# Second token chunk transposed by DMA instead of TensorE, first loads in another order, and two additions placed between scaling pieces

## Chip, core and metric

One NeuronCore of a Trainium2 chip runs the whole kernel. The metric is the device time of one execution in microseconds (us), lower is better. Engines are named as in the profile: PE is TensorE (matmuls), PEld its weight loads, DVE is VectorE, ACT is ScalarE, POOL is GpSimd; SP is SyncE, which here only issues DMAs. A name with a q (SPq, DVEq) is the engine's sequencer. L12 is line 12 of the kernel before.

## What is computed

2048 tokens of width 1024, bfloat16. A gate mixes two branches: a dilated local attention (8 keys per query, distance 2) and a gated feed-forward of width 3584.

```python
x = A_x                                                   # [1, 2048, 1024]
g = sigmoid((x * gate_w).sum(-1, keepdims=True))
q, k, v = split(x @ wqkv)                                 # 32 heads of 32
a = softmax_over_8_keys(q, k) @ v  ->  heads joined  @ wo
b = (gelu(x @ w_gate) * (x @ w_up)) @ w_down
out = g * a + (1 - g) * b
```

## The kernel before, in words

**Layout.** All matmuls contract over partitions, so x is needed transposed: features on the partitions, tokens along the row. The 2048 tokens are four chunks of 512, c = 0 to 3. A transposed chunk has eight slices (kt = 0 to 7) of 128 features by 512 tokens. Chunks 0 and 1 form `xf[0]` (tiles `c1`, `c2`), chunks 2 and 3 form `xf[1]`. Chunks 0 and 1 are loaded as they stand (`load_xn`, L141) and transposed on PE, 32 transposes of 128 x 128 each, with eight copies out of PSUM shared by DVE (L219) and ACT (L217) (`pe_transpose_chunk`, L208). Chunks 2 and 3 are transposed by DMA: 16 transposing DMAs of 512 tokens x 128 features from SP (L340).

**Units.** After a plain start (`plain_pair`, L240: the first 256 gate and up columns for chunks 0 and 1 by ordinary matmuls), projections run as "units" (class `Unit`, L360) with seven block products instead of eight (a Strassen-Winograd scheme). A unit has five PE steps. `p1` and `p5` are 4 matmuls each, `p26` is 8, `p73` is 8, `p4` is 4. PE's order is p1 of unit b, p73 of unit b-1, p5 and p26 of unit b, p4 of unit b-1. Between p73 and p4 of the same unit DVE reads the two PSUM banks with L403, and p4 adds into one of those banks, so p4 has to wait for L403. The units need sums and differences of the x blocks (`x_forms`, L196, line L199: T1 = R12 - R11, T2 = R22 - T1, T4 = R21 - T2, where R11 and R21 are slices 0-3 and 4-7 of the pair's first chunk, R12 and R22 those of its second) and of the weights (`sums_pair`, L318; `sums_qk`, L456, line L463). DVE makes the forms of `xf[1]` early, between the unit work of `xf[0]` (`late_forms`, L780).

**Order of the work.** Every engine runs its instructions in program order, written out by hand at the start and then by a planner: background DVE tasks with priorities and due units are cut into the units by credits (`run_bg`, L442). Loads are issued by SP, in order; stores by POOL. SP's order at the start: chunk 0, first weight pair in two column halves (`load_pair(raw0, 0, True)`, L172), chunk 1, second weight pair (L174), four q/k weight blocks of 1 MB (L336), 16 DMA transposes (L340), and then loads of `w_down` pieces (L860).

**End.** The second half of the down projection (`down(1)`, L1066) runs two-level block products (`level2`, L1037). For this half DVE makes all forms: `scale_task` (L918) multiplies a block of A by (1 - g) in three pieces of four slices, `comb_task` (L927) adds or subtracts blocks, `forms_L` and `forms_R` (L1004, L1012) make the inner sums. `join` (L1031) adds an inner product that is kept in SBUF to two PSUM banks, for i = 0 and i = 1; both wait for a product of PE. `pieces`, `take(g, k)` and `run` draw the next steps of such a chain: `rest` at L1093 holds the three scaling pieces of A21 and then the five pieces of AD = A11 - A21.

## Time and profile before

| | |
|---|---|
| median of 3 runs | 720.85 us (720.46 to 720.87) |
| profiled execution: its time, its span | 720.8 us, 719.0 us |
| PE busy | 707.4 us (98% of the span) |
| DVE busy | 673.0 us (94%) |
| ACT, POOL busy | 328.5 us, 134.1 us |
| moved by DMA | 162 MB, 225 GB/s mean |

A profile page gives the busy time of each engine, its load over the span in 40 slices, and groups of instructions by line: how many, mean length, and how long the engine stood idle before them and for whom. The timeline lists instructions in order of start, neighbours of a kind merged (x8); a number in brackets is idle time before, with the engine that ended it. A DMA line of SPq is the issue alone, the data land later. The two numbers at the head of a timeline row are start and length in us.

### The profile page before, as it was taken

What the parts mean: (1) busy time and instruction counts of PE and PEld (TensorE: products, weight loads), DVE (VectorE), ACT (ScalarE), POOL (GpSimd) and SP (SyncE); (2) the same over time, 40 slices, a digit from 0 to 9 for tenths busy, and PEclk for the clock granted to TensorE, in tenths of its full rate; (3) what the DMA queues carried; (4) which work ended last, traced back from release to release, by engine and by line L of the source; (5) the groups of instructions that cost most, each with busy time, mean ns of one, the idle gap of its engine ahead of it and who ended that gap; (6) DMA issues with size and microseconds to landing.
All of it is one profiled execution on the core that took longest, in us unless ns stands there. A gap on an engine that the chain in (4) does not pass through costs nothing. (4 is left out here: it accounts for less than half of the span.)

```text
span 719.0 us, 10748 instructions
## 1 busy us (share of the span) xinstructions
PE 707.4 (98%) x4051; PEld 408.3 (57%) x4107; DVE 673.0 (94%) x721; ACT 328.5 (46%) x600; POOL 134.1 (19%) x233
## 2 busy tenths in 40 slices
PE   8999999999999999999999999999999999999997
PEld 4466656655544444444444444444447886758886
DVE  2789989999999999999999999999999999899997
ACT  4554546444456665555555555555322321231421
POOL 1323544133210332121200000000210002110011
PEclk9999999999999999999999999999999999999999
DMA  9976743278264758574935746371891799995941
GB/s 276 283 176 227 229 142 133 98 248 303 100 206 128 234 190 254 171 227 142 294 111 155 279 134 210 120 285 59 314 421 60 301 405 399 422 427 217 379 196 60
DMA packets 91748, 162.04 MB, mean 225 GB/s; under 512 B 19264, under 2 KB 68320, under 8 KB 87344
## 3 DMA queue, kind: packets, MB, share of 16 engines
q1 hardware_dynamic: 74992, 105.46, 43.0%
q0 software_dynamic: 15984, 48.29, 19.3%
q10 hardware_dynamic: 720, 7.60, 2.7%
q8 instruction: 32, 0.52, 0.3%
q14 instruction: 20, 0.16, 0.1%
HBM read 112.17 MB, written 54.14 MB: 231 GB/s over the span
## 5 line engine op out<-in xcount | busy, mean ns | idle before, releaser
L366 PE MATMUL banks<-arena 128*128 128x512 bf16 x2136 | 472.1, 379 | 4.2 <-DVE arena L403 0.7
L366 PEld LDWEIGHTS <-arena 128*128 128x128 bf16 x2184 | 240.4, 111 | 235.3 <-issue 7.0
L1046 PE MATMUL banks<-arena 128*128 128x256 bf16 x1260 | 138.7, 273 | 0.6 <-DVE arena L1012 0.6
L1046 PEld LDWEIGHTS <-arena 128*128 128x128 bf16 x1260 | 123.1, 98 | 16.4 <-issue 1.1
L403 DVE TENSOR_TENSOR arena<-banks,arena 128x1024 bf16<-128x1024 f32 x78 | 95.2, 1221 | 11.0 <-PE banks L366 5.4
L389 ACT COPY arena<-banks 128x512 f32<-128x512 f32 x78 | 45.7, 586 | 130.8 <-PE banks L366 130.8
L374 ACT CAST arena<-banks 128x512 bf16<-128x512 f32 x102 | 59.6, 584 | 42.4 <-PE banks L366 42.4
L745 DVE TENSOR_TENSOR arena<-arena 128x2048 bf16<-128x2048 bf16 x64 | 77.0, 1220 | 0.5
L752 DVE TENSOR_TENSOR arena<-arena 128x2048 bf16<-128x2048 bf16 (+2 forms) x96 | 73.9, 776 | 1.0
L598 DVE TENSOR_TENSOR arena<-arena 128x2048 bf16<-128x2048 bf16 x64 | 74.7, 1219 | 0.1
L1075 PE MATMUL banks<-arena 128*128 128x512 bf16 x282 | 62.5, 379 | 0.3
L260 POOL DMA_DIRECT2D h_d<-arena x28 | 20.4, 728 | 226.6 <-DVE arena L254 195.5
L396 ACT COPY banks<-banks 128x512 f32<-128x512 f32 x78 | 44.5, 570 | 21.9 <-PE banks L366 20.1
L1004 DVE TENSOR_TENSOR arena<-arena 128x2304 bf16<-128x2304 bf16 x40 | 53.3, 1352 | 0.5
L384 ACT COPY banks<-banks 128x512 f32<-128x512 f32 x78 | 45.0, 576 | 13.6 <-PE banks L366 12.1
L1051 ACT COPY banks<-banks 128x256 f32<-128x256 f32 x60 | 21.4, 356 | 60.1 <-PE banks L1046 59.9
L1075 PEld LDWEIGHTS <-arena 128*128 128x128 bf16 x288 | 28.2, 98 | 33.6
L927 DVE TENSOR_TENSOR arena<-arena 128x2048 bf16<-128x2048 bf16 (+1 forms) x40 | 41.8, 1112 | 1.6 <-DMA arena<-h_d 1.6
L372 ACT ACTIVATE arena<-banks 128x512 bf16<-128x512 f32 x54 | 32.2, 597 | 15.4 <-PE banks L366 15.4
L323 DVE TENSOR_TENSOR arena<-arena 128x1024 bf16<-128x1024 bf16 x60 | 38.7, 685 | 0.5
L1012 DVE TENSOR_TENSOR arena<-arena 128x2304 bf16<-128x2304 bf16 x28 | 37.7, 1352 | 0.2
L254 DVE TENSOR_TENSOR arena<-arena 128x2048 bf16<-128x2048 bf16 x28 | 34.1, 1216 | 1.9 <-ACT arena L251 1.4
(90 smaller groups left out, 435.4 us busy)
## 6 DMA issues: line engine op xcount, KB each, us to landing
arena<-t_d SPq DMA_DIRECT2D x8, 2304.0 KB, 14.8
h_d<-arena POOLq DMA_DIRECT2D x28, 512.0 KB, 4.3
arena<-w_c SPq DMA_DIRECT2D x12, 1152.0 KB, 13.4
t_d<-arena POOLq DMA_DIRECT2D x36, 256.0 KB, 4.3
arena<-h_d SPq DMA_DIRECT2D x6, 1536.0 KB, 11.8
arena<-in_B_w_gate_dram SPq DMA_DIRECT2D x15, 512.0 KB, 5.7
arena<-in_B_w_up_dram SPq DMA_DIRECT2D x15, 512.0 KB, 4.9
arena<-in_B_w_down_dram SPq DMA_DIRECT2D x28, 256.0 KB, 6.7
```

The costliest lines, as they stand in the source:

```text
L366: self.pe = nc.tensor.matmul(ps, lhsT=self.L[form](kt), rhs=rhs[:, kt, :], start=(start and kt == 0), stop=(kt == HK - 1), skip_group_chec ...
L374: nc.scalar.copy(out=o_, in_=i_)
L384: nc.scalar.copy(out=self.Y, in_=self.X)
L389: nc.scalar.copy(out=self.p5s, in_=self.V)
L396: nc.scalar.copy(out=self.Z, in_=self.Y)
L403: TT(out=self.T[:, :, c2s], in0=pair, in1=self.p5s.rearrange("p (o n) -> p o n", o=1).to_broadcast([P, 2, SC]), op=ALU.add)
L598: TT(out=dst, in0=q.rearrange("p (o s) -> p o s", o=1).to_broadcast([P, NWIN, AC]), in1=_win_ap(k, [[-DIL, NWIN], [1, AC]]), op=ALU.mult)
L745: TT(out=prod2[(t // 2) % 2][:, t % 2], in0=ab, in1=_win_ap(v[:, t, HALO:HALO + AC], [[SJ, NJ], [-DIL, NWIN], [1, SJ]]), op=ALU.mult)
L752: TT(out=out_, in0=h(0), in1=h(1), op=ALU.add)
L1004: TT(out=o_, in0=a, in1=b_, op=op)
L1046: nc.tensor.matmul(c(i, h, j), lhsT=l[:, kt, j * P:(j + 1) * P], rhs=r[:, kt, :], start=False, stop=(kt == KH - 1), skip_group_check=True)
L1075: nc.tensor.matmul(ps, lhsT=L[:, i, j * P:(j + 1) * P], rhs=R[:, i, :], start=(start and q == 0), stop=(q == NK - 1), skip_group_check=not ...
```

## The change

Chunk 1 is no longer loaded as it stands (four loads of 256 KB) and transposed on PE; eight transposing DMAs from SP bring it instead, through the new function `load_xt`, which also does chunks 2 and 3. The first loads come in this order on SP: chunk 0, first column half of the first weight pair, slices 0 and 1 of chunk 1, second column half, slices 2 to 7 of chunk 1, second weight pair, q/k weights (now the k columns first), chunks 2 and 3. On PE `patterns()` (one small transpose) goes ahead of the first plain products, and the gate product of chunk 0 ahead of the plain products of chunk 1. In `down(1)` two scaling pieces instead of one go ahead of the first `join`, and one goes between the two.

```diff
-        def load_pair(dst, i, split=False):
+        def load_pair(dst, i, cols=((0, 2 * P),)):
             c0 = 2 * P * i
-            for (a, b) in (((0, P), (P, 2 * P)) if split else ((0, 2 * P),)):
+            for a, b in cols:
...
-        load_pair(raw0, 0, True)
-        load_xn(1)
-        load_pair(raw1, 1)
+        load_pair(raw0, 0, ((0, P),))
...
+        def load_xt(c, k0, k1):
+            dst = (xf[c // 2].c1, xf[c // 2].c2)[c % 2]
+            for kt in range(k0, k1):
+                nc.sync.dma_start_transpose(out=dst[:, kt, :], in_=x[c * SC:(c + 1) * SC, kt * P:(kt + 1) * P])
+
+        load_xt(1, 0, 2)
+        load_pair(raw0, 0, ((P, 2 * P),))
+        load_xt(1, 2, KT)
+        load_pair(raw1, 1)
...
-        for i, (col, k0) in enumerate(((0, 0), (0, HK), (D, 0), (D, HK))):
+        for i, col, k0 in ((2, D, 0), (3, D, HK), (0, 0, 0), (1, 0, HK)):
...
         for c in range(2, 4):
-            dst = (xf[1].c1, xf[1].c2)[c - 2]
-            for kt in range(KT):
-                nc.sync.dma_start_transpose(out=dst[:, kt, :], in_=x[c * SC:(c + 1) * SC, kt * P:(kt + 1) * P])
+            load_xt(c, 0, KT)
         G0, U0 = st_tile(), st_tile()
         pe_transpose_chunk(0, xf[0].c1)
+        patterns()
         plain_pair(raw0, G0, U0, 0, 0, xf[0].c1)
-        patterns()
-        pe_transpose_chunk(1, xf[0].c2)
+        gate_chunk(0, bank(6))
         list(x_forms(0))
         list(sums_pair(raw1, sums1))
         plain_pair(raw0, G0, U0, 0, 1, xf[0].c2)
-        for c in range(2):
-            gate_chunk(c, bank(6 + c))
+        gate_chunk(1, bank(7))
...
                 rest = pieces(scale_task(A21, s, 1, 0, NE_), comb_task(AD, A11, A21, ALU.subtract))
+                take(rest, 2)
+                join(XT, B["L1"], 0)
                 take(rest, 1)
-                joins(XT, B["L1"])
+                join(XT, B["L1"], 1)
```

## The prediction

> **What bounds the kernel now.** The page first: the busy shares.

> ```profile
> span 719.0 us, 10748 instructions
> PE 707.4 (98%) x4051; PEld 408.3 (57%) x4107; DVE 673.0 (94%) x721; ACT 328.5 (46%) x600; POOL 134.1 (19%) x233
> ```

> PE is the bound and almost never stops, so a change pays only if it takes work off PE or ends one of its few stops, and any new wait of PE is lost for good. DVE comes next, at 94%. Then the places that the change touches, in the timeline. PE at the start:

> ```profile
> 14.57 2.33 PE L213 MATMUL banks<-ident,arena 128*128 128x128 bf16 x32
> 17.14 1.89 PE L245 MATMUL banks<-arena 128*128 128x512 bf16 x7 [0.25 <-DVE arena L219]
> 18.87 1.89 PE L249 MATMUL banks<-arena 128*128 128x512 bf16 x8
> ...
> 25.12 1.25 PE L366 MATMUL banks<-arena 128*128 128x512 bf16 x4
> ```

> The 32 transposes of chunk 1 hold PE from 14.56 to 17.14. Units begin at 25.12. Eight matmuls take 1.73 (18.87 to the next group at 20.59), 0.216 each.

> SP's issues at the start:

> ```profile
> 1.69 0.43 SPq L167 DMA_DIRECT2D arena<-in_B_w_gate_dram  x1
> 2.15 0.58 SPq L167 DMA_DIRECT2D arena<-in_B_w_up_dram  x1
> 2.78 3.02 SPq L167 DMA_DIRECT2D arena<-in_B_w_gate_dram  x1
> 5.84 1.00 SPq L167 DMA_DIRECT2D arena<-in_B_w_up_dram  x1
> 6.88 2.66 SPq L143 DMA_DIRECT2D arena<-in_A_x_dram  x4
> 9.59 0.43 SPq L167 DMA_DIRECT2D arena<-in_B_w_gate_dram  x1
> ...
> 16.00 29.81 SPq L340 DMA_TRANSPOSE arena<-in_A_x_dram  x16
> ```

> A load costs SP some 0.4 to 0.6 us; the third weight half takes 3.02 because the queue ahead of it is full. The 16 transposes fill SP to 45.81. Asked for its last two, line L340 says that even without a queue ahead each keeps SP 1.26 us (start to start 1.305 with the gap) and lands 2.6 after its start:

> ```profile
> L340 SPq DMA_TRANSPOSE arena<-in_A_x_dram x2: 1258/1259/1260, 43.2 to 44.6; - x2
> ...
> DMA to landing us min/median/max: 2.6/2.6/2.7
> ```

> So a transpose of 128 KB moves at 100 GB/s at best, set by SP's issue, while the DMA row of the windows from 18 to 26 us shows plain loads at 381 to 393 GB/s. The last transpose lands at 44.56 + 2.6 = 47.2. Its reader on DVE:

> ```profile
> L199 DVEq EVENT_SEMAPHORE  x4: 21/50/2655, 44.3 to 47.2; - x4
> ...
> 46.60 3.74 DVE L199 TENSOR_TENSOR arena<-arena 128x2048 bf16<-128x2048 bf16 x3
> 50.26 1.22 DVE L403 TENSOR_TENSOR arena<-banks,arena 128x1024 bf16<-128x1024 f32 x1
> ...
> 53.62 0.59 ACT L374 CAST arena<-banks 128x512 bf16<-128x512 f32 x1 [0.29 <-PE banks L366]
> ```

> DVE's sequencer stands 2.66 us ahead of time at the semaphores of these forms, until 47.2, the landing. The second of the three (T2) reads the last chunk's upper slices and starts at 46.60 + 1.25 = 47.85: 0.65 us to spare, no more. Last, the end, where `join` waits:

> ```profile
> 627.50 0.70 DVE L1031 TENSOR_TENSOR banks<-banks,arena 128x512 f32<-128x512 f32 x1 [1.94 <-PE banks L1046]
> 629.47 0.70 DVE L1031 TENSOR_TENSOR banks<-banks,arena 128x512 f32<-128x512 f32 x1 [1.27 <-PE banks L1046]
> 630.08 2.35 DVE L918 TENSOR_TENSOR arena<-arena,omgrep 128x2048 bf16<-128x2048 bf16 x2
> ...
> 663.36 4.87 PE L1046 MATMUL banks<-arena 128*128 128x256 bf16 x43 [0.62 <-DVE arena L1012]
> ```

> DVE idles 1.94 and 1.27 us ahead of the two joins, has the two left scaling pieces at 630.08, then works without a break, and at 663.36 PE waits for its form.

> **The change, part by part.** *The joins.* The two scaling pieces (2.35 / 2 = 1.17 each) go into idle stretches of 1.94 and 1.27; both fit, so everything on DVE behind them comes 2.35 earlier. PE's stop at 663.36 needs less: 0.62 of idle time is 0.79 between starts (the matmul before begins at 662.47, the pitch is 0.11). A wait on data takes its place only if an operand is late; the buffer that the form at 661.96 writes is last read by PE 6 x 18 matmuls of 0.109 after 644.74, at 656.5, clear of 659.6. **-0.8 us**; ends 0 and -0.9.

> *PE's transposes.* Off PE: 17.14 - 14.56 = 2.6. The eight copies (DVE and ACT) vanish and were not on the path. `patterns` moves ahead: its small transpose costs 0.1 wherever it stands; at 7.3 it may wait for `gwr`, 0 to 0.2. The gate product of chunk 0 only changes places (0.5).

> *The eight transposes on SP.* Slices 0 and 1 take the place of the third half load at 2.78, with the same queue ahead. When slice 2 can be issued no row shows. If nothing is held: 2 x 1.305 and two halves of 0.47 and 0.62 put it at 6.5. If slice 0 is held like the row of 3.02, and the second half again for 3.02 and 1.00: 5.80 + 1.3 + 4.1 = 11.2. I take 9.5: the queue is as full as in those rows, so nearer the late end. Slice 7 is then issued at 9.5 + 5 x 1.305 = 16.0 and lands at 18.6. PE arrives for it at 14.5 + 0.6 (gate product) + 1.5, so it waits some 2 us inside its first eight matmuls; then three groups (5.2) and the second gate product (0.8): the units start at 24.7, where it was 25.1. Most of the 2.6 is lost to this wait.

> *What stands behind on SP.* The second weight pair is issued at 17.3 instead of 9.59. It then has no queue ahead: 2.6 to landing as a transpose, plus 1.0 for the other 384 KB at 385 GB/s, is 20.9; before it landed 5.7 after issue, at 15.3. All behind it moves by 5.6: q/k weights, then chunks 2 and 3. The weights are in time: their readers L463 start at 29.19, when four blocks had landed; the k columns now come first, and two of four blocks at 23.7 + 5.6 = 29.3 suffice. The 16 transposes are not: the last lands at 47.2 + 5.6 = 52.8. T2 on DVE starts 5 us late (47.85), and behind it in DVE's order stand T4, L403, three L598 products, small memsets and L874. **PE waits for L403**: from T2's start to L403's end it is 51.48 - 47.85 = 3.63. The reader of PE's next step p4 starts at 53.62 (ACT L374), so p4 (4 matmuls, 3 x 0.216 + 0.38 for the last) begins at 52.55. Now it begins at 52.8 + 3.63 + 0.1 = 56.5. **+4.0 us** of PE, an absolute bound: the 0.4 gained before is swallowed by it, since it does not matter when PE comes to wait. In the next two units DVE has 6.1 of work per unit against 6.05 on PE, **+0.2**, before idle stretches of DVE (0.8 and 1.3 near 90 us) end the lag.

> `w_down` loads behind the transposes come 5.6 later too; their reader L874 at 55.30 comes 4 to 5 later itself and had 1.4 to spare: nothing, up to 0.5. The h store of POOL (issued at 31.09, 512 KB) now falls into the q/k loads: -0.4 to +1.4 on the landing, taken as 0.

> **Sum**, on the profiled execution's own time (720.8, of which 719.0 is span; the median is 720.85, the same): 720.8 - 0.8 + 4.0 + 0.2 = **724.2**. With slice 2 issued at 6.5 the last landing is 49.8 and the sum 721.2; at 11.2 it is 725.9, and 727.3 with the store.

> **Rivals.** *Transposes run at the pace of loads* (ends on the other side). If early transposes issue back to back as loads do, chunk 1 costs SP what its four loads cost (2.66), nothing behind it moves, the last landing stays at 47.2, and p4, which comes at 52.55 - 2.6 = 49.95, waits to 47.2 + 3.73 = 50.9: -1.6 - 0.8, 718.4. It decides if a transpose takes SP under 0.6 us. Against it: 1.26 in the rows above. [...]

> *The landing is late but in time.* If SP is held far less than in the rows and the last transpose lands by 49.6, the wait and the joins cancel: 720.8.

> *The clock drops.* PE's first six matmuls start 0.43 apart, later ones 0.216: after standing idle it ran at half pace, until 4.5 at the latest, some 3.3 us. A stop of 4 us may bring this again, once or twice: +1.6 to +3.3, 726.7. No stop after the start is longer than 0.62, so no row decides. [...]

> *The joins pay nothing*: 725.0, inside the first case.

> **How the numbers follow.** Late transposes 0.63 (721.9 to 726.2); clock drop on top 0.15; load-pace transposes 0.14; late but in time 0.08. Slower by over 0.2% (1.4 us, about what a measurement of this kernel can tell) is the first two, 0.77, less a little at the low end; same 0.09, faster 0.14. The range leaves out the fastest case: 719.4 to 728.0.

> **What would show it.** Right: SP's transposes of chunk 1 at 1.26 each to about 17; the group of 16 ending near 51; L199 split, its second part near 53; a PE stop of some 4 us at p4 there, ended by L403; no stop at the sixth form (663 + 4). Wrong: PE idle ahead of 25 us only, or L199 in one piece: then the landings were earlier than my queue reckoning, and the time falls toward 718 to 721.

## The result and the profile after

The changed kernel takes **728.08 us** (median of 4 runs, 726.81 to 728.78); the kernel before took 720.86 beside it (720.46 to 721.26). The ratio is **1.0098**, interval 1.0081 to 1.0116: about 1% slower, where 724.2 was forecast, just outside the range's upper end. The profiled run took 728.36 with a span of 726.6 (before: 720.8 and 719.0). One execution each of e4 (4320 us), e6 (2672 us) and the kernel before (746 us) was disturbed and is left out below. Each ratio is to the kernel before as measured beside that run (medians of 720.68 to 721.78). In the new kernel L366 is called L371, L403 L408, L199 L207, L340 L194, L598 L603, L874 L879, L1031 L1036 and L1046 L1051; in e6, e7 and e9 L371 and L408 are L379 and L416, in e10 L369 and L406.

The page of the changed kernel, its span and busy shares, and the clock that the throttle granted in 40 slices of 18.2 us:

```profile
span 726.6 us, 10738 instructions
PE 711.0 (98%) x4075; PEld 406.5 (56%) x4075; DVE 671.6 (92%) x717; ACT 326.7 (45%) x596; POOL 134.2 (18%) x233
PEclk9998999999999999999999999999999999999999
```

PE shows 3.6 us more busy time (711.0 against 707.4), though 32 transposes went. The 8 in the fourth slice (54.5 to 72.7 us) says part of why: there its clock was below full. The rest can't be read from these two figures, since matmul records are missing from the trace of before (2136 of 2184 for its L366). The timeline of the changed kernel, start and length in us, at the start:

```profile
9.24 8.20 SPq L194 DMA_TRANSPOSE arena<-in_A_x_dram  x6
17.49 0.59 SPq L167 DMA_DIRECT2D arena<-in_B_w_gate_dram  x1
19.20 0.38 PE L253 MATMUL banks<-arena 128*128 128x512 bf16 x1 [1.36 <-DMA arena<-in_A_x_dram]
23.30 30.34 SPq L194 DMA_TRANSPOSE arena<-in_A_x_dram  x16
25.23 17.93 PE L371 MATMUL banks<-arena 128*128 128x512 bf16 x82
```

Slices 2 to 7 go out from 9.24 on, PE waits 1.36 (and 0.42 at 17.46) for the last ones, and the units begin at 25.23, 0.11 later than before. SP comes to chunks 2 and 3 at 23.30 instead of 16.00. What that does, in the same timeline:

```profile
51.56 1.23 DVE L207 TENSOR_TENSOR arena<-arena 128x2048 bf16<-128x2048 bf16 x1 [4.71 <-DMA arena<-in_A_x_dram]
55.42 2.48 DVE L207 TENSOR_TENSOR arena<-arena 128x2048 bf16<-128x2048 bf16 x2 [2.63 <-DMA arena<-in_A_x_dram]
57.82 1.22 DVE L408 TENSOR_TENSOR arena<-banks,arena 128x1024 bf16<-128x1024 f32 x1
59.09 11.10 PE L371 MATMUL banks<-arena 128*128 128x512 bf16 x40 [6.20 <-DVE arena L408]
```

DVE idles 4.71 for T1 and 2.63 for T2, whose last slices landed at 55.30, instead of 47.16 before. L408 ends at 59.04, and p4 starts at 59.09 after **6.20 us in which PE stood still**. Before, p4 started at 52.56 without a stop, inside this row, whose one wait is at its start:

```profile
43.44 19.65 PE L366 MATMUL banks<-arena 128*128 128x512 bf16 x88 [0.43 <-DVE arena L463]
```

The clock of the changed kernel around its p4, in windows of half a microsecond (busy time of PE, PEld, DVE, ACT and POOL; then the granted clock, 1.00 being full; then DMA share and GB/s):

```profile
56.50:57.00 0.50, 0.00 (x0) 0.00 (x0) 0.47 (x2) 0.00 (x0) 0.00 (x0) 0.95 0.97 338
57.00:57.50 0.50, 0.00 (x0) 0.00 (x0) 0.50 (x1) 0.00 (x0) 0.00 (x0) 0.50 1.05 317
...
63.00:63.50 0.50, 0.50 (x3) 0.22 (x2) 0.50 (x1) 0.32 (x1) 0.14 (x1) 0.50 1.12 373
63.50:64.00 0.50, 0.50 (x4) 0.17 (x2) 0.03 (x1) 0.00 (x0) 0.00 (x0) 0.72 1.04 348
```

The clock falls to half inside the stop, at 56.95 (0.95 over the first window is half for a tenth of it), and returns at 63.78. From 59.09 on PE works through 4.69 us at half rate and loses half of that, **2.35 us**: about ten matmuls 0.43 apart instead of 0.216. At the end the stop of 0.62 us ahead of the sixth form is gone:

```profile
L1051 PE MATMUL banks<-arena 128*128 128x256 bf16 x1260 | 138.3, 273 | 0.0
```

The last figure is PE's idle time ahead of the line's matmuls. How far the changed kernel lags at the same step: 8.83 at the stop that stood at 118.55 before, 8.82 at the one at 509.93, 7.86 at the last copies of ACT out of PSUM (ACT's L1051 before, start 710.97; L1056 now, start 718.83). So the whole loss, 6.53 (p4 at 59.09 instead of 52.56) + 2.35 = 8.9, is made between 52 and 64 us, and the joins give back 0.96.

### The profile page after: what moved, and what is told of

The parts are those of the page before. It is cut to its first block, busy times and chain, and to the rows that moved or that the text cites. A ratio compares the mean times of both kernels' runs of the same rounds, so it can differ in the third digit from the quotient of the medians.

```text
span 726.6 us, 10738 instructions
## 1 busy us (share of the span) xinstructions
PE 711.0 (98%) x4075; PEld 406.5 (56%) x4075; DVE 671.6 (92%) x717; ACT 326.7 (45%) x596; POOL 134.2 (18%) x233
## 5 line engine op out<-in xcount | busy, mean ns | idle before, releaser
L371 PE MATMUL banks<-arena 128*128 128x512 bf16 x2184 | 477.3, 381 | 7.7 <-DVE arena L408 6.9
L371 PEld LDWEIGHTS <-arena 128*128 128x128 bf16 x2184 | 240.6, 111 | 243.8 <-issue 16.5
L1051 PE MATMUL banks<-arena 128*128 128x256 bf16 x1260 | 138.3, 273 | 0.0
L1051 PEld LDWEIGHTS <-arena 128*128 128x128 bf16 x1260 | 123.2, 98 | 15.3 <-issue 0.3
L408 DVE TENSOR_TENSOR arena<-banks,arena 128x1024 bf16<-128x1024 f32 x78 | 95.2, 1221 | 11.1 <-PE banks L371 5.8
L379 ACT CAST arena<-banks 128x512 bf16<-128x512 f32 x102 | 59.6, 584 | 43.4 <-PE banks L371 43.4
L603 DVE TENSOR_TENSOR arena<-arena 128x2048 bf16<-128x2048 bf16 x64 | 74.7, 1218 | 0.1
L1080 PE MATMUL banks<-arena 128*128 128x512 bf16 x288 | 62.8, 379 | 0.0
L401 ACT COPY banks<-banks 128x512 f32<-128x512 f32 x78 | 44.5, 570 | 28.1 <-PE banks L371 19.8
L389 ACT COPY banks<-banks 128x512 f32<-128x512 f32 x78 | 44.9, 576 | 14.5 <-PE banks L371 13.3
L1056 ACT COPY banks<-banks 128x256 f32<-128x256 f32 x60 | 21.4, 356 | 59.1 <-PE banks L1051 58.9
L1080 PEld LDWEIGHTS <-arena 128*128 128x128 bf16 x288 | 28.1, 98 | 33.6
```

Of the source, the lines that this page charges most:

```text
L371: self.pe = nc.tensor.matmul(ps, lhsT=self.L[form](kt), rhs=rhs[:, kt, :], start=(start and kt == 0), stop=(kt == HK - 1), skip_group_chec ...
L379: nc.scalar.copy(out=o_, in_=i_)
L389: nc.scalar.copy(out=self.Y, in_=self.X)
L401: nc.scalar.copy(out=self.Z, in_=self.Y)
L408: TT(out=self.T[:, :, c2s], in0=pair, in1=self.p5s.rearrange("p (o n) -> p o n", o=1).to_broadcast([P, 2, SC]), op=ALU.add)
L603: TT(out=dst, in0=q.rearrange("p (o s) -> p o s", o=1).to_broadcast([P, NWIN, AC]), in1=_win_ap(k, [[-DIL, NWIN], [1, AC]]), op=ALU.mult)
```

## The experiments

**Theory**: the last transpose lands late, the forms of chunks 2 and 3 wait for it ahead of L408 on DVE, and PE waits for L408, plus a time at half clock that the stop brings. **Rivals**: the new order at the front costs something by itself (units, unit buffers, DMA load); the joins cost something; the slow stretch is the price of other work (weight loads, DMA) and not of the stop.

**e1, the joins alone**, in the kernel before:

```diff
+                take(rest, 2)
+                join(XT, B["L1"], 0)
                 take(rest, 1)
-                joins(XT, B["L1"])
+                join(XT, B["L1"], 1)
```

> The kernel before with the two joins placed between the scaling pieces and nothing else. Theory (the joins end PE's stop at the sixth inner form, 0.79 us between starts): 720.1 us against 720.9, 0.7 to 0.8 less, and the idle time of 0.62 ahead of line L1046 is gone. Rival (another operand is late in its place): 720.9, with the stop under another name.

719.88 (719.59 to 721.62, 11 runs), ratio 0.9978 [0.9968, 0.9989], span 718.5. From the view of the timeline of e1 between 626 and 670 us:

```profile
645.27 24.99 PE L1046 MATMUL banks<-arena 128*128 128x256 bf16 x226
```

PE runs through the place (663 us) without a stop. The lag behind the kernel before turns from +0.52 at 509.93 (PE waited 0.5 longer at 7 us in this execution) to -0.45 at ACT's last copies: the joins are worth 0.97, as in the changed kernel.

**e2, the front alone**: the changed kernel with the old joins (the diff of e1 the other way round).

> The changed kernel with the joins put back as before. Theory (the whole loss is in the first loads; the joins gain 0.8 by themselves): 728.9 us, 0.8 over the changed kernel, with the stop of some 6.2 us at p4 and the stop of 0.6 us at the sixth inner form. Rival (parts of the loss come from the joins): 728.1 or less.

729.63 (728.24 to 730.28), ratio 1.0110 [1.0096, 1.0125], span 728.0; 0.7 more than expected. The stop at p4 is there (6.39), and the 0.62 at the sixth form is back (671.98 to 672.60). The front loses, the joins gain, and the two add up.

**e3, the forms later**: the task of the forms of chunks 2 and 3 wakes one unit later and that of the `w_down` forms (L879) two units later, so that L408 does not stand behind the wait.

```diff
-        due(Q0 + NT, bg(late_forms(), 3, Q0 + 1))
+        due(Q0 + NT, bg(late_forms(), 3, Q0 + 2))
...
-        tft = bg(t_forms(), 6, Q0 + 2)
+        tft = bg(t_forms(), 6, Q0 + 4)
```

> The changed kernel, but DVE's forms of chunks 2 and 3 may start one unit later (behind the three products of that unit), and the w_down forms two units later; the loads stay as they are. Theory (PE is lost only because L408, which p4 needs, stands on DVE behind forms whose last transpose lands at 55.3): no PE stop over 1 us after 25 us, no slow stretch, 720.1 to 720.8 us. Rival (the late loads themselves cost, wherever their reader stands; or the front is slower by itself): 724 us or more.

727.0 (725.18 to 730.63), ratio 1.0084 [1.0053, 1.0115]: missed. From two stretches of its timeline:

```profile
58.16 1.22 DVE L207 TENSOR_TENSOR arena<-arena 128x2048 bf16<-128x2048 bf16 x1 [2.18 <-DMA arena<-in_A_x_dram]
60.58 3.61 PE L371 MATMUL banks<-arena 128*128 128x512 bf16 x16 [1.83 <-DVE arena L408]
...
115.83 4.19 DVE L879 TENSOR_TENSOR arena<-arena 128x1024 bf16<-128x1024 bf16 x6
...
125.89 4.43 PE L371 MATMUL banks<-arena 128*128 128x512 bf16 x13 [3.17 <-DVE arena L408]
```

The stop at the first p4 goes, and 1.83 of it comes at the next. But what DVE put off has to be done by its due unit: six L879 in a row at 115.83 push an L408 back and PE stops for 3.17, with half clock from 125.47 to 128.89. Idle time of DVE near 50 us is work that is missing later.

**e4, the stop filled with matmuls** that go into an unused bank and are read by nobody; nothing else is touched:

```diff
+            if b == 4:
+                for i in range(24):
+                    nc.tensor.matmul(bank(6), lhsT=xf[0].c1[:, 0, 0:P], rhs=xf[0].c1[:, 0, :], start=True, stop=True)
             if prv:
```

> The changed kernel with 24 extra matmuls into an unused bank ahead of the p4 that waits (5.2 us of PE work inside the stop of 6.4 us; their product is read by nobody). Theory (after the stop PE runs about ten matmuls at half pace because it stood idle): the stop of PE shrinks to about 1.2 us behind the extra matmuls, p4 starts at the same 59.1, the matmuls after it start 0.216 apart, and the time falls by about 2.1 us to 726.0. Rival (the slow stretch has another cause, such as late operands): ten matmuls 0.43 apart stay, 728.1 us.

726.43 (726.34 to 727.40, 3 runs), ratio 1.0073 [1.0057, 1.0088], span 724.6, granted clock 1.0 throughout. Its timeline:

```profile
53.27 5.34 PE L1252 MATMUL banks<-arena 128*128 128x512 bf16 x24
59.35 4.91 PE L371 MATMUL banks<-arena 128*128 128x512 bf16 x22 [0.74 <-DVE arena L408]
```

p4 starts as late as before (59.35, last landing 55.56), but 22 matmuls take 4.91 where the changed kernel made some twelve in that time. The span is 2.0 shorter, with p4 0.26 later: 2.3, the 2.35 that the clock's rows gave. The slow stretch is the price of the stop, not of the work after it.

**e5, the first h store from SP, behind the transposes** (`h_store(G0, U0, 0, 0, nc.sync)` instead of POOL), to see what it costs the loads.

> The changed kernel with the first h store (512 KB, issued by POOL at 28.1) moved to SP's queue behind the 16 transposes. Theory (this store falls into the last q/k block, which landed 3.6 us behind the one before it instead of 2.7, and with it moves all transposes): the fourth q/k block and the last transpose land about 1 us earlier (36 and 54.3), PE's stop at p4 is 5.3 instead of 6.4 us, 727 us. Rival (the store slips in beside the transposes for nothing): stop and time as in the changed kernel.

739.78 (738.36 to 740.51), ratio 1.0259 [1.0242, 1.0275]. Its time does not answer: the tile that is stored is needed again by the units, so ACT (idle 18.30 until the DMA into h_d has landed) and PE wait for the store.

```profile
56.16 6.00 PE L371 MATMUL banks<-arena 128*128 128x512 bf16 x16 [17.18 <-ACT banks L389]
```

A stop of 17.18 us; half clock from 43.96 to 61.02. Its landings do answer: POOL issues no DMA between 33.8 and 65.5 us here, the last q/k block lands at 36.09 and the last transpose at 53.07 (expected 36 and 54.3), each of the last ones 2.7 after its issue. The first store's own price comes from e8.

**e6 and e7, two and four slices of chunk 1 by DMA**, the other six and four loaded as they stand and transposed on PE (`KD` = 2 or 4):

```diff
-        load_xt(1, 2, KT)
+        if KD > 2:
+            load_xt(1, 2, KD)
+        for j in range(4):
+            nc.sync.dma_start(out=xn[1][:, j, KD * P:D], in_=x[SC + j * P:SC + (j + 1) * P, KD * P:D])
...
         gate_chunk(0, bank(6))
+        pe_transpose_chunk(1, xf[0].c2, KD)
```

> The changed kernel, but only slices 0 and 1 of chunk 1 come by transposing DMA; the other six are loaded as they stand (four loads of 192 KB) and transposed on PE (24 transposes). Theory (each slice by DMA moves the last landing of chunks 2 and 3 by about 1 us, and PE has 1.7 us to spare there): last landing near 48.7, a stop of at most 0.6 us at p4, no slow stretch, 719.6 to 720.4 us. Rival (it is the first transposes among plain loads that cost, or the new order as such): a stop of several us, 724 us or more.

> The same with four slices by DMA and four on PE (16 transposes). Theory: last landing near 51, the stop at p4 2 to 3.5 us, too short for a slow stretch, 721.5 to 723.5 us: between two slices and eight. Rival (a threshold elsewhere): as two slices, or as eight.

e6: 721.21 (720.19 to 721.77, 9 runs), ratio 1.0004 [0.9995, 1.0014]; the stop came out as expected, the time 0.8 above the range, with a p4 1.4 later than before. e7: 727.06 (720.94 to 727.99, 10 runs), ratio 1.0074 [1.0054, 1.0093], missed because it landed later than expected and the clock fell (e3 lost it at a stop of 3.17, inside the 2 to 3.5 that was expected to be too short). The p4 rows, e6 first, then e7:

```profile
53.98 8.36 PE L379 MATMUL banks<-arena 128*128 128x512 bf16 x38 [0.31 <-DVE arena L416]
```

```profile
56.67 5.51 PE L379 MATMUL banks<-arena 128*128 128x512 bf16 x14 [4.37 <-DVE arena L416]
```

The last transposes landed at 50.19 and 52.88. Fewer transposes on SP, earlier landing, shorter stop: the effect grows with the dose, as the theory has it.

**a0, the changed kernel again**, beside these:

> The changed kernel once more, as the mark for the three kernels beside it: 728 us.

727.96 (727.19 to 730.68), ratio 1.0106 [1.0078, 1.0133]; stop 6.08, last landing 54.96, half clock from 54.84 to 61.67.

**e8, the first two h stores cut to an eighth** (the rest of those rows of h is written later from other data, so these blocks are not the reference's):

```diff
-            nc.gpsimd.dma_start(out=h_d[s][e][:, :, i0 // 2, :], in_=flat(G).rearrange("p (hc s) -> p hc s", hc=4))
+            nn = SC // 8 if s == 0 and i < 2 else SC
+            nc.gpsimd.dma_start(out=h_d[s][e][:, :, i0 // 2, 0:nn], in_=flat(G).rearrange("p (hc s) -> p hc s", hc=4)[:, :, 0:nn])
```

> The changed kernel with the two h stores that run beside the early loads cut to an eighth (64 KB instead of 512 KB; the rest of these h rows is filled later with other data, so two of the blocks that the down projection reads are wrong). Theory (the stores take DMA time from the last q/k block and from the transposes): last q/k block at 35.5 to 36.3 instead of 36.8, last transpose 53 to 54 instead of 55.1, PE's stop at p4 4.2 to 5.3 us, 726 to 727 us. Rival (the stores fit into gaps): 55 and 728.

726.77 (726.42 to 728.0), ratio 1.0073 [1.0056, 1.0090]. The last q/k block lands at 35.73 (a0 36.73, the changed kernel 36.94), the last transpose at 53.28 (54.96 and 55.30), and the stop is 4.34. The two stores of 512 KB hold the loads up by 1.0 to 1.2 and the last transpose by 1.7 to 2.0.

**e9 and e11, two tasks of DVE exchanged**: the forms of chunks 2 and 3 wake a unit later, and the three L603 products that stood behind them a unit earlier, so that DVE has work in the wait. e9 has it on e7, e11 on the changed kernel:

```diff
-        due(Q0 + NT, bg(late_forms(), 3, Q0 + 1))
+        due(Q0 + NT, bg(late_forms(), 3, Q0 + 2))
...
-                due(n_ + 4, bg(qk_prods(units[n_], s, t), 2, n_ + 2))
+                due(n_ + 4, bg(qk_prods(units[n_], s, t), 2, n_ + 2 - (n_ == Q0)))
```

> Four slices by DMA as before, and on DVE the forms of chunks 2 and 3 change places with the three products L603 of the unit before, which read finished data; every other instruction keeps its place. Theory (only the place of the waiting forms ahead of L408 costs): no stop over 0.5 us after 20 us, no slow stretch, PE 1 us earlier at the start: 719.0 to 720.2 us, at or below the joins alone. Rival (the late landing costs wherever its reader stands): 724 or more.

> The changed kernel with nothing but that exchange on DVE: the three products of the unit before ahead of the forms of chunks 2 and 3. The last transpose still lands near 55. Theory: the stop of 6.2 us and the slow stretch are gone, at most 0.6 us is left at the next p4, 720.2 to 721.2 us, the level of the kernel before. Rival (late loads cost wherever their reader stands): 724 or more.

e9: 719.97 (719.43 to 720.58, 12 runs), ratio 0.9977 [0.9968, 0.9986], where e7 had 727.06. Its timeline:

```profile
48.08 3.50 DVE L611 TENSOR_TENSOR arena<-arena 128x2048 bf16<-128x2048 bf16 x3 [1.51 <-ACT arena L387]
51.50 1.22 DVE L416 TENSOR_TENSOR arena<-banks,arena 128x1024 bf16<-128x1024 f32 x1
...
52.77 9.25 PE L379 MATMUL banks<-arena 128*128 128x512 bf16 x41 [0.16 <-DVE arena L416]
54.29 2.48 DVE L211 TENSOR_TENSOR arena<-arena 128x2048 bf16<-128x2048 bf16 x2 [0.44 <-DMA arena<-in_A_x_dram]
```

Its last transpose landed at 54.17, **later** than e7's, and PE does not stop: the products fill the wait, and L416 (L408) is no longer behind the forms. e11: 721.95 (720.75 to 728.47, 12 runs), ratio 1.0015 [0.9994, 1.0036]. It missed: at most 0.6 was expected to be left at the next p4. There the landing is 56.28, the forms run at 56.41, and the next L408 comes late for the next p4 (61.98, a stop of 2.52). Two of its twelve runs, 727.01 and 728.47, show a clock of 0.998 and 0.994, the others 1.0 or nearly.

**e10, the kernel before with three more transposes** (into a spare region, ahead of the 16), its order otherwise untouched:

```diff
+        spare = reg3(116, 3, SC)
+        for kt in range(3):
+            nc.sync.dma_start_transpose(out=spare[:, kt, :], in_=x[SC:2 * SC, kt * P:(kt + 1) * P])
         for c in range(2, 4):
```

> The kernel before with three extra transposing DMAs into an unused region ahead of the 16 (3 x 1.305 = 3.9 us later for these), all else as it was. Theory (the landing alone sets the loss): last transpose at 51.1, L408's counterpart ends 3.7 later, PE's stop at p4 2.0 to 2.6 us, too short for a slow stretch, 723.0 to 723.6 us. Rival (the loss needs the new order of the first loads): 721 us.

726.51 (726.08 to 727.48), ratio 1.0068 [1.0052, 1.0084]: 3 above the expected. The landing was expected at 51.1 and came at 53.04, so the stop was 3.83 and not 2.0 to 2.6, and the clock fell. Why it came late is argued, not shown: POOL's stores of 45.99 to 48.87, the second h store among them, now stand beside the last transposes (last section). The mechanism is the theory's, without anything of the new front. The p4 row, and then the clock in half microseconds:

```profile
56.84 7.46 PE L369 MATMUL banks<-arena 128*128 128x512 bf16 x26 [3.83 <-DVE arena L406]
```

```profile
57.50:58.00 0.50, 0.50 (x4) 0.36 (x3) 0.50 (x2) 0.10 (x1) 0.50 (x2) 1.00 1.10 350
58.00:58.50 0.50, 0.50 (x3) 0.23 (x2) 0.50 (x1) 0.50 (x3) 0.50 (x2) 0.58 1.09 346
...
61.00:61.50 0.50, 0.50 (x2) 0.17 (x1) 0.28 (x1) 0.00 (x0) 0.00 (x0) 0.51 1.07 378
```

PE is back at 56.84 at full clock, and only at 58.08 does the clock fall, while PE is busy; it returns at 61.49.

**Together.** In eight kernels p4 starts 3.73 us after the last landing, plus 0.06 or 0.07. And the span follows from three numbers: 719.0, plus p4's start less 52.56, plus half of the time that PE worked at half clock, less 0.97 where the joins are changed:

| kernel | last landing | + 3.73 | p4 starts | half clock while PE works | span worked out | span |
|---|---|---|---|---|---|---|
| changed | 55.30 | 59.03 | 59.09 | 4.69 | 726.9 | 726.6 |
| a0 | 54.96 | 58.69 | 58.75 | 2.92 | 725.7 | 726.3 |
| e2 | 55.24 | 58.97 | 59.03 | 4.92 | 727.9 | 728.0 |
| e4 | 55.56 | 59.29 | 59.35 | 0 | 724.8 | 724.6 |
| e6 | 50.19 | 53.92 | 53.98 | 0 | 719.5 | 719.3 |
| e7 | 52.88 | 56.61 | 56.67 | 4.75 | 724.5 | 724.2 |
| e8 | 53.28 | 57.01 | 57.08 | 4.76 | 724.9 | 724.6 |
| e10 | 53.04 | 56.77 | 56.84 | 3.41 | 725.0 | 724.8 |
| e9 | 54.17 | not behind it | 52.77 | 0 | 718.2 | 718.2 |

All within 0.6; a0, the furthest, has a further stop of 0.5 at 588 us. The rivals fall: a front with four slices by DMA costs nothing once the stop is gone (e9; with all eight, e11, a smaller stop was left), the joins gain (e1), and the slow stretch belongs to the stop (e4). e1 and e9 beat both kernels, the kernel before by 0.2% (ratios 0.9978 and 0.9977), and they are the same within what was measured: the 16 transposes that e9 takes off PE buy nothing that shows.

## Why the prediction was wrong, step by step

The sign and the mechanism held; the time missed by 3.9, and nearly all of it is two steps.

- *The joins, -0.8*: right in sign and cause; -0.96 in the changed kernel and -0.97 in e1, just past the end of -0.9.
- *PE's transposes and chunk 1 on SP*: right. Slice 2 was issued at 9.24 (forecast 9.5), slice 7 at 16.18 (16.0) and landed at 19.16 (18.6); the units start at 25.23 (24.7). That 9.5 hit is partly luck: of the two holds behind the late end, 11.2, slice 0 showed one of 3.87 and the second weight half none (0.58 and 0.57). That a full queue makes these holds was the author's reading of the row of 3.02; no run tried it. The forecast's point that a later wait makes this time worthless holds as well. The rival of transposes at the pace of loads is out: from slice 2 on they start 1.3 apart or more, as the row of before had it. But the 100 GB/s are the pace of SP's issue alone: transposes that had queued up behind the q/k blocks landed 0.5 to 0.7 apart (37.36, 38.06, 38.68, 39.16).
- *"All behind it moves by 5.6"*: **the step that failed**. It moved by 8.1 (47.16 to 55.30), so the stop made p4 6.53 later instead of 4.0. In parts: the second weight pair's first load landed 4.5 after issue, at 22.00, not 3.4 to 3.6 after, at 20.9 (+1.1). The four q/k blocks took 13.2 from there (23.72 to 36.94) where they took 12.0 before (17.06 to 29.10): +1.2. With the first h store of POOL cut (e8) they take 12.4, with it moved away (e5) 12.1, so 0.8 to 1.2 of it is this store, which the prediction named, bounded (-0.4 to +1.4) and took as 0. (It was issued at 28.13 and shows on the third and fourth block. The first block is 1.2 late for a cause that isn't shown, and in the kernel before the second was late by as much.) The last 0.3 is behind that. Why the weight pair took 4.5 is not shown; four small stores of POOL (issued 16.57 to 18.07) fell beside it, and that was not tried alone.
- *p4 at the landing + 3.63 + 0.1*: right to 0.07 in eight kernels.
- *DVE as the bound for two units, +0.2*: not seen; p4 and the clock make 8.88, and at 127 us the lag is 8.83.
- *The clock*: taken as a rival with a chance of 0.15 and left out of the sum. The chance was the author's estimate: after PE's start no row of before holds a stop over 0.62. It came with the stop of 6.2, 2.35 of the 3.9, and the forecast's 4 us would have been no safer by these runs: the clock fell with stops of 3.17 (e3), 3.83 (e10), 4.34 (e8) and 4.37 (e7) as well.

On the profiled execution: 724.2 + 2.5 (p4) + 2.35 (clock) - 0.15 (joins) - 0.2 (DVE's bound) = 728.7; it took 728.36, and 0.3 stays without a place.

## What to carry to other kernels

A load that is moved ahead on a queue is paid by everything behind it: follow the queue to the reader with the least slack (here 0.65 us at 47.85) and count for the delay every other transfer that it will now meet, not the moved instructions alone. On a PE that never stops, price a stop at its length plus half clock (here 1.5 to 2.5 us behind every profiled stop of 3.17 us or more, nothing behind those of 2.52 and less), and look for other work of the waiting engine that can go ahead of the wait (e9 removed 7 us by exchanging two tasks). Idle time of a nearly full engine isn't free to take either: what is put off comes back at its due time (e3).

## What the runs showed of the hardware

**Stores of POOL are paid by SP's loads.** With the first store cut from 512 to 64 KB (e8) the last q/k block landed 1.0 to 1.2 earlier; 448 KB at the 385 GB/s of the prediction's rows are 1.2. A load that is delayed can so meet a store that it was clear of: in e10 three transposes of 1.305, 3.9 in all, moved the last landing by 5.9. The second h store is one candidate by its place, but it isn't alone: with it cut to an eighth (e8) the transposes issued at 46.47 and 47.79 still landed 4.7 after issue, beside POOL's smaller stores, and with none of POOL's stores there (e5) all those issued from 37.34 on landed 2.7 to 2.8 after issue. None of these stores was moved alone, and in e5 PE stood still as well.
